# An exp split over two engines: VectorE's share as fp16 bits in six passes instead of seven, with an offset row in Q and K, and a new instruction order

## The chip, the cores and the metric

One core of one Trainium2 chip. The metric is the device time of one execution in microseconds, the median of several. Engines: PE is TensorE, DVE is VectorE, ACT is ScalarE.

## The reference

Two independent halves on inputs of 2048 x 640, joined at the end. Half A is a 2-D FFT filter, done in the kernel as chains of matmuls. Half B is attention with 32 heads of width 20:

```python
qkv = (x @ wqkv).reshape(B, S, 3, H, Dh)...          # H = 32, Dh = 20, S = 2048
scores = einsum("bhqd,bhkd->bhqk", q, k) * Dh ** -0.5
p = softmax(scores, axis=-1)
o = einsum("bhqk,bhkd->bhqd", p, v)
return o.transpose(...).reshape(B, S, D) @ wo
```

The exps of the softmax are the bulk: 32 x 2048 x 2048 of them, 2048 tiles of 128 keys by 512 queries.

## The kernel before

A scheduler in the program places every instruction of every engine in a fixed order, from estimated durations; the chip then runs each engine's queue in that order, with semaphores between them. PE makes scores of two or three tiles at a time into PSUM ("qk"), ACT takes their exp in one instruction into one of four SBUF buffers (PT), PE multiplies them with V ("PV") into one PSUM bank that belongs to the unit (four heads by 512 queries); at a unit's end DVE copies the bank out, and only then may the next unit's PV start. The exp on ACT, with scale and bias as immediates (the bias is the default 0):

```python
self.P.add("act", lambda e: e.activation(pt, in_, AF.Exp, scale=SCALE),
           r=[("ps", h + k) for k in range(n)], w=[("PT", i % 4)], name="exp")
```

DVE does some of the exps itself, two tiles at a time ("a pair"). It writes 1024*log2(e)*score as a uint16, corrects the fraction bits by a polynomial, and turns the sum into bits of a 16-bit float:

```python
# x_v: from PSUM, twice per pair
tensor_scalar(v, ps, 1024 * SCALE * LOG2E, 32 * 1024 + 512, mult, add)
# then on 128x1024 in SBUF, 16 bits:
x_s: sh = v << 6
x_t: t = sh * a + b                 # tensor_scalar
x_q: h = t * t                      # tensor_tensor
x_l: t = t * c + d                  # tensor_scalar
x_h: h = h * t                      # tensor_tensor
x_w: v = v + h                      # tensor_tensor
x_p: v = v * 0.125 + X_BIAS         # tensor_scalar: to bits of bf16
```

Evictions of Q and K from PSUM are plain casts (`copy_on`). All DVE jobs of half A (among them the complex multiply of stage FS2) are placed between these passes.

## Time and profile before

| | before |
|---|---|
| time, median | 916.43 us (915.7 to 918.68) |
| ACT busy | 839.7 us, of it exps 828.8 us (724 instructions) |
| DVE busy | 815.7 us |
| ACT idle ahead of exps | 53.4 us |
| granted PE clock, mean | 0.963 |

How to read it: in a group line, the first number after the bar is the union of the busy time, the second the mean duration of one instruction in ns, the third the idle time of its engine just before it and what ended most of it. Where records of one engine overlap, the union is less than count times duration. A hole is a stretch in which ACT waits. One piece of the trace belongs here: the 9.33 us hole, in time order (start, length, engine, line, operation).

```profile
564.09 0.61 PE L1265 MATMUL ps<-arena 128*128 128x512 bf16 x2 [2.58 <-DVE arena L227]
...
564.88 1.41 DVE L1253 TENSOR_TENSOR arena<-ps,arena 128x512 f32<-128x512 f32 x2
...
565.17 0.62 PE L1879 MATMUL ps<-arena 128*21 128x512 bf16 x4
566.21 0.68 DVE L1903 COPY arena<-ps 128x512 f32<-128x512 f32 x1
...
567.32 1.04 PE L1879 MATMUL ps<-arena 128*32 128x512 bf16 x8
...
567.99 1.45 ACT L1714 ACTIVATE arena<-ps 128x1536 bf16<-128x1536 f32 x1 [9.33 <-PE ps L1879]
```

Read it upwards. The exp waits for a PT buffer, which eight PVs of the new unit free (L1879). They wait for the copy of the old unit's bank (L1903). The copy comes after the old unit's last PVs (565.17) and, on DVE, after two multiplies of FS2 (L1253). Those PVs in turn stand on PE behind a matmul of half A (L1265), for which PE waited 2.58 us until DVE had done a cast (L227). So lateness on DVE, which is full of FS2 work, reaches ACT in steps, at a unit's end.

### The profile page before, as it was taken

To read this page: it belongs to the slowest core of one execution; us is meant where nothing else is said; L and a number is where in the kernel's file an instruction comes from. 1 tells how busy PE (TensorE), PEld (TensorE's weight loads), DVE (VectorE), ACT (ScalarE), POOL (GpSimd) and SP (SyncE) were. 2 spreads that over 40 slices of the span, in tenths; PEclk is the share of its full clock that TensorE was granted. 3 is DMA by queue.
4 is the path that set the end of the run, shared out by engine and by line. 5 is a ranking of instruction groups with operands and counts; after the bars stand their busy time and mean duration, and the time that the engine had idled before them with its cause. 6 is when DMAs were issued, how large, how long until landed. Compare 5 with 4: busy or idle time off the path is not lost.

```text
span 915.7 us, 16468 instructions
## 1 busy us (share of the span) xinstructions
PE 837.9 (92%) x6731; PEld 291.2 (32%) x6823; DVE 815.7 (89%) x1642; ACT 839.7 (92%) x744; POOL 2.9 (0%) x7
## 2 busy tenths in 40 slices
PE   8999999999899999999999997898899998989986
PEld 4433333333233333322233322223233332223222
DVE  5797799999799998999899999999999898678994
ACT  6898999998799999999999995999799999789993
POOL 1000000000000000000000000000000000000000
PEclk9999999999699999999999998999799999679999
DMA  7430000003200000011001000010010201011100
GB/s 228 87 82 14 2 14 13 14 14 93 73 28 27 13 14 13 14 48 36 13 20 35 13 13 1 13 59 14 1 59 20 78 13 42 1 41 43 42 13 32
DMA packets 31830, 31.85 MB, mean 35 GB/s; under 512 B 13444, under 2 KB 26500, under 8 KB 31492
## 3 DMA queue, kind: packets, MB, share of 16 engines
q1 hardware_dynamic: 31748, 30.73, 11.2%
q8 instruction: 55, 0.90, 0.4%
q14 instruction: 27, 0.22, 0.1%
HBM read 24.97 MB, written 5.50 MB: 33 GB/s over the span
## 4 chain that ended last, share of the span: by engine, by line
ACT 52%; PE 21%; DVE 20%; DMA 5%; issue 1%; SPq 0%; ACTq 0%; DVEq 0%
ACT arena L1714 51%; PE ps L1697 6%; DVE arena L227 4%; DMA arena<-rscr 4%; PE ps L1879 4%; DVE arena L1787 3%; DVE arena L1253 2%; PE ps L1331 2%; DVE arena L1828 1%; DVE arena L1835 1%; DVE arena L1832 1%; PE ps L1596 1%; DVE arena L1258 1%; PE ps L1533 1%; PE ps L1583 1%
## 5 line engine op out<-in xcount | busy, mean ns | idle before, releaser
L1714 ACT ACTIVATE arena<-ps 128x1536 bf16<-128x1536 f32 x724 | 828.8, 1276 | 53.4 <-PE ps L1697 28.2
L1697 PE MATMUL ps<-arena 32*128 32x512 bf16 x2048 | 309.3, 394 | 42.4 <-ACT arena L1714 22.5
L1879 PE MATMUL ps<-arena 128*32 128x512 bf16 (+1 forms) x2048 | 208.3, 401 | 5.0 <-DVE arena L1837 2.2
L1787 DVE TENSOR_SCALAR arena<-ps 128x512 uint16<-128x512 f32 x238 | 163.4, 687 | 30.6 <-PE ps L1697 28.4
L227 DVE CAST arena<-ps 128x512 bf16<-128x512 f32 (+4 forms) x248 | 143.7, 580 | 22.6 <-PE ps L1331 6.1
L1697 PEld LDWEIGHTS ps<-arena 32*128 32x128 bf16 x2048 | 74.3, 91 | 247.9 <-ACT arena L1714 180.7
L1879 PEld LDWEIGHTS ps<-arena 128*32 128x32 bf16 (+1 forms) x2048 | 51.3, 92 | 132.4 <-issue 107.6
L1583 PE MATMUL ps<-arena 128*128 128x512 bf16 x244 | 85.3, 397 | 3.5 <-issue 2.4
L1828 DVE TENSOR_TENSOR arena<-arena 128x1024 f16<-128x1024 f16 x119 | 81.8, 687 | 1.1
L1832 DVE TENSOR_TENSOR arena<-arena 128x1024 f16<-128x1024 f16 x119 | 81.9, 688 | 0.9
L1835 DVE TENSOR_TENSOR arena<-arena 128x1024 uint16<-128x1024 uint16 x119 | 81.5, 685 | 0.6
L1826 DVE TENSOR_SCALAR arena<-arena 128x1024 f16<-128x1024 int16 x119 | 50.4, 424 | 0.8
L1830 DVE TENSOR_SCALAR arena<-arena 128x1024 f16<-128x1024 f16 x119 | 50.1, 421 | 0.9
L1824 DVE TENSOR_SCALAR arena<-arena 128x1024 uint16<-128x1024 uint16 x119 | 50.1, 422 | 0.4
L1837 DVE TENSOR_SCALAR arena<-arena 128x1024 uint16<-128x1024 uint16 x119 | 50.1, 421 | 0.4
L1533 PE MATMUL ps<-arena 128*32 128x512 bf16 x640 | 47.8, 381 | 1.2 <-issue 0.5
L1596 PE MATMUL ps<-arena 128*128 128x512 bf16 x145 | 46.5, 396 | 1.5 <-issue 0.8
L1331 PE MATMUL ps<-arena 128*128 128x320 bf16 (+1 forms) x192 | 43.0, 330 | 4.3 <-DVE arena L1787 4.2
L227 DVE COPY arena<-ps 128x1024 bf16<-128x1024 bf16 (+2 forms) x55 | 40.2, 733 | 6.0 <-PE ps L540 4.6
L1583 PEld LDWEIGHTS ps<-arena 128*128 128x128 bf16 x317 | 26.7, 98 | 44.9 <-issue 39.3
L1964 PE MATMUL ps<-arena 128*128 128x320 bf16 x192 | 38.2, 303 | 0.1
L1942 DVE TENSOR_TENSOR arena<-arena 128x512 bf16<-128x512 f32 x31 | 21.4, 689 | 15.9 <-DMA arena<-rscr 15.4
(71 smaller groups left out, 464.3 us busy)
## 6 DMA issues: line engine op xcount, KB each, us to landing
arena<-rscr SPq DMA_DIRECT2D x31, 256.0 KB
arena<-in_B_x_dram SPq DMA_DIRECT2D x4, 640.0 KB, 6.4
arena<-in_A_x_dram SPq DMA_DIRECT2D x4, 640.0 KB, 6.2
out_dram<-arena SPq DMA_DIRECT2D x16, 160.0 KB, 1.8
out_dram<-arena SPq DMA_DIRECT2D x4, 640.0 KB, 3.4
arena<-f_ciCS SPq DMA_DIRECT2D x2, 1024.0 KB, 5.1
arena<-arena SPq DMA_DIRECT2D x124, 2.0 KB, 1.7
arena<-f_cslab SPq DMA_DIRECT2D x2, 768.0 KB, 4.4
```

The lines of the kernel that those rows point to most:

```text
L227: return eng.tensor_copy(out, in_)
L1331: return lambda e: e.matmul(o, l, r_, start=s_, stop=e_)
L1533: inst = e.matmul(ps[32 * j:32 * j + 32, bank, :], self.wqkv[:, cbv, c:c + 32], r_, start=st, stop=sp, tile_position=(0, 32 * j))
L1583: self.P.add("pe", lambda e: e.matmul(ps[:, 6, :], z, k[:, 0, 0:512], start=False, stop=False, skip_group_check=True), r=[("KT", 0, 0), (" ...
L1596: return lambda e: e.matmul(o, l, r_, start=st, stop=sp)
L1697: inst = e.matmul(ps[:, bank, :], kt_[32 * j:32 * j + 32, g, kt * 128:(kt + 1) * 128], q[32 * j:32 * j + 32, :], start=True, stop=True, ti ...
L1714: self.P.add("act", lambda e: e.activation(pt, in_, AF.Exp, scale=SCALE), r=[("ps", h + k) for k in range(n)], w=[("PT", i % 4)], name="exp")
L1787: self.P.add("dve", lambda e: e.tensor_scalar(v, in_, 1024.0 * SCALE * LOG2E, 32.0 * 1024 + 512, ALU.mult, ALU.add), r=[("ps", bank)], **( ...
L1828: t = self.x_op(n, two, lambda e: e.tensor_tensor(h16, t16, t16, ALU.mult), [ka], [kb], "x_q")
L1832: t = self.x_op(n, two, lambda e: e.tensor_tensor(h16, h16, t16, ALU.mult), [ka, kb], [kb], "x_h")
L1835: t = self.x_op(n, two, lambda e: e.tensor_tensor(v, v, h16, ALU.add), [kb, kv], [kv], "x_w")
L1879: inst = e.matmul(ps[32 * j:32 * j + m, 6, :], va[:, kt, 21 * h:21 * h + m], pt, start=st, stop=sp, tile_position=(0, 32 * j))
```

## The change

Its intent: take a pass off DVE, which is nearly full, by letting the scores carry an offset, so that x_v already gives the bits of fp16 (whose exponent bias is 15) and x_p falls away; and order the queues by measured durations. The offset is an added row, 1 in K and 46.5 in Q: 46.5 * SCALE is 15 in units of log2. ACT, which reads the same scores, takes it off again by its bias. The bias, and the scale and bias of the added row, come from columns of a small tile kq: one value for each of the 128 partitions, [128,1], in place of a constant in the instruction (an immediate).

```diff
+        kq[:, 0] = kq[:, 2] = 1.0
+        kq[20::32, 0:4] = (0.0, 1.0, 0.0, Y_ROW)     # scale, bias of K; scale, bias of Q
+        kq[:, 4] = -15.0 / LOG2E
...
+    def add_row(self, e, en, out, in_, c):           # replaces copy_on for Q and K
+        m, b = self.kq[:, c:c + 1], self.kq[:, c + 1:c + 2]
+        if en == "act":
+            return e.activation(out, in_, AF.Identity, bias=b, scale=m)
+        return e.tensor_scalar(out, in_, m, b, ALU.mult, ALU.add)
...
-        e.activation(pt, in_, AF.Exp, scale=SCALE)
+        e.activation(pt, in_, AF.Exp, scale=SCALE, bias=self.kq[:, 4:5])
...
-        x_v: ... 1024.0 * SCALE * LOG2E, 32.0 * 1024 + 512, ALU.mult, ALU.add
+        x_v: ... 1024.0 * SCALE * LOG2E, 31743.0, ALU.mult, ALU.min
...        (x_t, x_q, x_l, x_h: other coefficients; x_q is now uint16 * fp16)
-        elif step == 6: ... tensor_scalar(v, v, 0.125, X_BIAS, mult, add)    # x_p
...        (order)
-        FS2: 1.0417 * ne + 64               +  ... + 124 and + 144
-        UT evictions 0.52 ns an element     +  1.0417
-        job on DVE: sum + 40.0              +  sum + 3.0
+        a PV may start with fewer than four tiles when ACT would else be stuck
-        T_A=680000.0, WIN=1000.0, T_X=0.0, (wait for rb 3600.0)
+        T_A=760000.0, WIN=1400.0, T_X=40000.0, T_RB=9000.0
```

The names of the order part: FS2 and UT are stages of half A, "job on DVE" is what the scheduler adds to each DVE job; T_A paces half A, WIN is the stretch by which the scheduler decides on filler matmuls, T_X the earliest time of DVE's exps, T_RB the wait before a unit's normalization. The sums' certificate, a check of their range (max and min in two reduces, now one), changes too.

More of the change, by code (lines that the diff above doesn't have):

```diff
@@ L1122, in mkev @@
                         return lambda e, en: copy_on(e, en, o, in_)
-                    ev = [(mkev, 0.833 * n * 128 + 63, 0.52 * n * 128 + 64, [], [dst_key(c, b0 // 8)] + zwr, [])]
+                    ev = [(mkev, 0.833 * n * 128 + 63, (1.0417 if tag == "UT" else 0.52) * n * 128 + 64, [], [dst_key(c, b0 // 8)] + zwr, [])]
                     aft = after[c] if isinstance(after, dict) else after
@@ L1253, in mkev @@
                     return lambda e, en: e.tensor_tensor(t[k], ps[:, bank, 0:ne], w, ALU.mult)
-                return (mkev, 0.0, 1.0417 * ne + 64, kw, [("tmp", k)] + zw("K", 2), [])
+                return (mkev, 0.0, 1.0417 * ne + 124, kw, [("tmp", k)] + zw("K", 2), [])
             def comb(y, k0, k1, op, key, t=t):
@@ L1258, in mkev @@
                     return lambda e, en: e.tensor_tensor(y, t[k0], t[k1], op)
-                return (mkev, 0.0, 1.0417 * ne + 64, [("tmp", k0), ("tmp", k1), zr("K", 2)], [key] + zw("B", 3), [])
+                return (mkev, 0.0, 1.0417 * ne + 144, [("tmp", k0), ("tmp", k1), zr("K", 2)], [key] + zw("B", 3), [])
             for co in range(2):
@@ L1370 @@
 LOG2E = 1.4426950408889634
-X_K, X_BETA, X_GAMMA = 18.8641107, -0.0282624809, 0.224521806
-X_BIAS = 12084.9708
+Y_ROW = 46.5
+X_A, X_B = 0.30457565, 0.07826797
 MODE = 100.0
 SLACK = 200.0
+F16 = mybir.dt.float16
 DMA_NS = 2200.0
@@ L1415, in alloc @@
         self.outB = [a.bf(take(1280), 640) for _ in range(2)]
-        self.rin = a.f32(take(64), 16)
-        self.rc = a.f32(take(64), 16)
+        self.rr = a.f32(take(128), 32)
+        self.rin, self.rc = self.rr[:, 0:16], self.rr[:, 16:32]
+        self.kq = a.f32(take(32), 8)
         self.mm = a.f32(take(256), 64)
         self.cert = a.f32(take(32), 8)
-        self.flagt = a.f32(take(32), 8)
+        self.flagt = self.cert[:, 6:8]
         self.vmx = a.f32(take(64), 16)
@@ L1462, in setup_B @@
         self.dma(self.ident, cBd.ap(), w=[("ident",)], name="ld_ident")
+        kq = np.zeros((128, 8), np.float32)
+        kq[:, 0] = kq[:, 2] = 1.0
+        kq[20::32, 0:4] = (0.0, 1.0, 0.0, Y_ROW)
+        kq[:, 4] = -15.0 / LOG2E
+        kqd = self.nc.inline_tensor(kq, self.prefix + "kq")
+        self.dma(self.kq, kqd.ap(), w=[("kq",)], name="ld_kq")
         xB = self.B_x[0].rearrange("(t p) c -> p t c", p=128)
@@ L1539, in mk_jobs_B_static, with mkev @@
                 J.pe = pe
+                def mkev(bank, g=g, kc=kc):
+                    o = self.KT[:, g, kc * 512:(kc + 1) * 512]
+                    return lambda e, en: self.add_row(e, en, o, ps[:, bank, :], 0)
+                J.ev = [(mkev, 490.0, 600.0, [("kq",)], [("KT", g, kc)], [])]
                 J.mode = "c"
@@ L1600, in mkev @@
             o = self.QA[u % 2]
-            in_ = ps[:, bank, :]
-            return lambda e, en: copy_on(e, en, o, in_)
-        ev = [(mkev, 490.0, 598.0, [], [("QA", u % 2)], [])]
+            return lambda e, en: self.add_row(e, en, o, ps[:, bank, :], 2)
+        ev = [(mkev, 490.0, 600.0, [("kq",)], [("QA", u % 2)], [])]
         cond = lambda p: g in self.wq_done and (u < 2 or self.qk_left[u - 2] == 0)
@@ L1713, in try_exp @@
         in_ = self.ps[:, h:h + n, :].rearrange("p b n -> p (b n)")
-        self.P.add("act", lambda e: e.activation(pt, in_, AF.Exp, scale=SCALE),
-                   r=[("ps", h + k) for k in range(n)], w=[("PT", i % 4)], name="exp")
+        self.P.add("act", lambda e: e.activation(pt, in_, AF.Exp, scale=SCALE, bias=self.kq[:, 4:5]),
+                   r=[("ps", h + k) for k in range(n)] + [("kq",)], w=[("PT", i % 4)], name="exp")
         t = self.occupy("act", 512 * n * 0.8333 + 50.0, 0.0)
@@ L1786, in try_x_first @@
         key = ("xv", n % NXV)
-        self.P.add("dve", lambda e: e.tensor_scalar(v, in_, 1024.0 * SCALE * LOG2E, 32.0 * 1024 + 512, ALU.mult, ALU.add),
+        self.P.add("dve", lambda e: e.tensor_scalar(v, in_, 1024.0 * SCALE * LOG2E, 31743.0, ALU.mult, ALU.min),
                    r=[("ps", bank)], **({"w": [key]} if k == 0 else {"pw": [key]}), name="x_v")
@@ L1808, in try_x_step @@
             self.x_step(c)
-            if c[1] == 7:
+            if c[1] == 6:
                 self.x_run.remove(c)
@@ L1815, in x_step @@
         n, step, t, pair = c
-        I16, F16 = mybir.dt.int16, mybir.dt.float16
         kv, ka, kb = ("xv", n % NXV), ("xa", n % 2), ("xb", n % 2)
         xv, xa, xb = self.xv[n % NXV], self.xa[n % 2], self.xb[n % 2]
-        v, sh, g = xv.bitcast(U16), xa.bitcast(U16), xa.bitcast(I16)
-        t16, h16 = xa.bitcast(F16), xb.bitcast(F16)
+        v, sh = xv.bitcast(U16), xa.bitcast(U16)
+        a16, b16 = xa.bitcast(F16), xb.bitcast(F16)
         one, two = 336.0, 603.0
@@ L1825, in x_step @@
         elif step == 1:
-            t = self.x_op(n, one, lambda e: e.tensor_scalar(t16, g, X_K / 65536.0, X_K * X_BETA, ALU.mult, ALU.add), [ka], [ka], "x_t")
+            t = self.x_op(n, one, lambda e: e.tensor_scalar(b16, sh, -2.0 ** -24, 2.0 ** -8, ALU.mult, ALU.add), [ka], [kb], "x_l")
         elif step == 2:
-            t = self.x_op(n, two, lambda e: e.tensor_tensor(h16, t16, t16, ALU.mult), [ka], [kb], "x_q")
+            t = self.x_op(n, two, lambda e: e.tensor_tensor(b16, sh, b16, ALU.mult), [ka, kb], [kb], "x_q")
         elif step == 3:
-            t = self.x_op(n, one, lambda e: e.tensor_scalar(t16, t16, X_GAMMA / X_K, 1.0 - X_GAMMA * X_BETA, ALU.mult, ALU.add), [ka], [ka], "x_l")
+            t = self.x_op(n, one, lambda e: e.tensor_scalar(a16, sh, -4.0 * X_B / 65536.0, -4.0 * X_A, ALU.mult, ALU.add), [ka], [ka], "x_l")
         elif step == 4:
-            t = self.x_op(n, two, lambda e: e.tensor_tensor(h16, h16, t16, ALU.mult), [ka, kb], [kb], "x_h")
+            t = self.x_op(n, two, lambda e: e.tensor_tensor(b16, b16, a16, ALU.mult), [ka, kb], [kb], "x_h")
             self.xa_free[n % 2] = t
         elif step == 5:
-            t = self.x_op(n, two, lambda e: e.tensor_tensor(v, v, h16, ALU.add), [kb, kv], [kv], "x_w")
-        elif step == 6:
-            t = self.x_op(n, one, lambda e: e.tensor_scalar(v, v, 0.125, X_BIAS, ALU.mult, ALU.add), [kv], [kv], "x_p")
+            t = self.x_op(n, two, lambda e: e.tensor_tensor(v, v, b16, ALU.add), [kb, kv], [kv], "x_w")
             for k, (u, kt, j) in enumerate(pair):
-                self.pv_ready[u].append((t + SLACK, kt, j, xv[:, 512 * k:512 * k + 512], kv))
+                self.pv_ready[u].append((t + SLACK, kt, j, xv.bitcast(F16)[:, 512 * k:512 * k + 512], kv))
             self.at(t + SLACK)
@@ L1860, in try_pv @@
                 break
-        if len(pick) < min(least, self.pv_left[u]):
+        heads = sum(self.pv_cnt.get((u, j), 0) < 16 for j in range(4))
+        i = self.nexp
+        stuck = i < self.nqk and self.qk_t[i] <= self.now and self.pt_free[i % 4] > self.now + 1e9 and self.tf["act"] <= self.now
+        if len(pick) < (1 if stuck else min(least, heads)):
             return False
@@ L1921, in unit_recip @@
         P.add("dve", lambda e: e.reciprocal(rc, rin), r=[("rin",)], w=[("rc",)], name="recip")
-        m0, m1 = self.mm[:, 2 * u:2 * u + 1], self.mm[:, 2 * u + 1:2 * u + 2]
-        P.add("dve", lambda e: e.tensor_reduce(m0, rin, AX.X, ALU.max), r=[("rin",)], pw=[("mm",)], name="smax")
-        P.add("dve", lambda e: e.tensor_reduce(m1, rin, AX.X, ALU.min), r=[("rin",)], pw=[("mm",)], name="smin")
-        t = self.occupy("dve", 400.0)
+        m, both = self.mm[:, 2 * u:2 * u + 2], self.rr.rearrange("p (c e) -> p c e", c=2)
+        P.add("dve", lambda e: e.tensor_reduce(m, both, AX.X, ALU.max), r=[("rin",), ("rc",)], pw=[("mm",)], name="sums")
+        t = self.occupy("dve", 270.0)
         rs = self.rscr[u]
@@ L1934, in d2 @@
             self.dma(rb, src, r=[("rs", u)], w=[("rb",)], stream="rb", name="rb")
-            self.dve_urgent.append((self.now + 3600.0, lambda: self.unit_norm(u), lambda: self.op_left[:u // NG].count(0) == u // NG))
-            self.at(self.now + 3600.0)
+            self.dve_urgent.append((self.now + self.cfg["T_RB"], lambda: self.unit_norm(u), lambda: self.op_left[:u // NG].count(0) == u // NG))
+            self.at(self.now + self.cfg["T_RB"])
         self.at(t, d1)
@@ L2031, in tail_norm @@
         if qb == 3:
-            m0, m1, ball = self.mm[:, 62:63], self.mm[:, 63:64], self.ps[:, 5, :]
-            self.P.add("dve", lambda e: e.tensor_reduce(m0, ball, AX.X, ALU.max), r=[("ps", 5)], pw=[("mm",)], name="smax")
-            self.P.add("dve", lambda e: e.tensor_reduce(m1, ball, AX.X, ALU.min), r=[("ps", 5)], pw=[("mm",)], name="smin")
+            m0, m1, ball, inv = self.mm[:, 62:63], self.mm[:, 63:64], self.ps[:, 5, :], self.rb
+            self.P.add("dve", lambda e: e.tensor_reduce(m0, ball, AX.X, ALU.max), r=[("ps", 5)], pw=[("mm",)], name="sums")
+            self.P.add("dve", lambda e: e.tensor_reduce(m1, inv, AX.X, ALU.max), r=[("rb",)], pw=[("mm",)], name="sums")
     def tail_act(self):
@@ L2141, in try_bg_ev @@
                            r=[("ps", J.bank)] + list(rk), w=wk, pw=pk, name=J.name + ".ev")
-            t = self.occupy(en, sum(x[1 if en == "act" else 2] for x in J.ev) + 40.0)
+            t = self.occupy(en, sum(x[1 if en == "act" else 2] for x in J.ev) + (40.0 if en == "act" else 3.0))
             J.done_p = t
@@ L2305, in emit_flag @@
         ps = self.ps
-        LO, HI = 2.0 ** -8, 2.0 ** 31
-        P.add("dve", lambda e: e.tensor_reduce(c[:, 0:1], mm, AX.X, ALU.max), r=[("mm",)], w=[("c", 0)], name="cmax")
-        P.add("dve", lambda e: e.tensor_reduce(c[:, 1:2], mm, AX.X, ALU.min), r=[("mm",)], w=[("c", 1)], name="cmin")
+        both = mm.rearrange("p (u c) -> p c u", c=2)
+        P.add("dve", lambda e: e.tensor_reduce(c[:, 0:2], both, AX.X, ALU.max), r=[("mm",)], w=[("c", 0)], name="csum")
         P.add("dve", lambda e: e.tensor_reduce(c[:, 2:3], self.vmx, AX.X, ALU.max), r=[("vmx",)], w=[("c", 2)], name="cv")
-        P.add("dve", lambda e: e.tensor_single_scalar(c[:, 3:4], c[:, 0:1], HI, ALU.is_gt), r=[("c", 0)], w=[("c", 3)], name="f0")
-        P.add("dve", lambda e: e.tensor_single_scalar(c[:, 4:5], c[:, 1:2], LO, ALU.is_lt), r=[("c", 1)], w=[("c", 4)], name="f1")
-        P.add("dve", lambda e: e.tensor_single_scalar(c[:, 5:6], c[:, 2:3], 2.0 ** 60, ALU.is_gt), r=[("c", 2)], w=[("c", 5)], name="f2")
+        P.add("dve", lambda e: e.tensor_single_scalar(c[:, 3:4], c[:, 0:1], 65000.0, ALU.is_le), r=[("c", 0)], w=[("c", 3)], name="f0")
+        P.add("dve", lambda e: e.tensor_single_scalar(c[:, 4:5], c[:, 1:2], 2.0 ** -6, ALU.is_le), r=[("c", 0)], w=[("c", 4)], name="f1")
+        P.add("dve", lambda e: e.tensor_single_scalar(c[:, 5:6], c[:, 2:3], 2.0 ** 60, ALU.is_le), r=[("c", 2)], w=[("c", 5)], name="f2")
         o1 = self.ones1
@@ L2315, in emit_flag @@
               r=[("c", 3), ("c", 4), ("c", 5), ("ones1",)], w=[("ps", 7)], name="fsum")
-        P.add("dve", lambda e: e.tensor_reduce(fl[0:1, 1:2], ps[0:1, 7, 0:3], AX.X, ALU.max), r=[("ps", 7)], w=[("fl", 1)], name="fmax")
+        P.add("dve", lambda e: e.tensor_reduce(fl[0:1, 1:2], ps[0:1, 7, 0:3], AX.X, ALU.min), r=[("ps", 7), ("c", 5)], w=[("fl", 1)], name="fmin")
         fi = fl.bitcast(mybir.dt.int32)[0:1, 0:1]
-        self.flag_task = P.add("dve", lambda e: e.tensor_single_scalar(fi, fl[0:1, 1:2], 0.0, ALU.is_gt), r=[("fl", 1)], w=[("fl", 0)], name="flag")
+        self.flag_task = P.add("dve", lambda e: e.tensor_single_scalar(fi, fl[0:1, 1:2], 127.5, ALU.is_lt), r=[("fl", 1)], w=[("fl", 0)], name="flag")
         self.flag = fi
@@ L2341, in bass_concat_heads__spectral_gfnet__softmax_full_mha__prompt_kernel @@
     arena = Arena(nc, 212832 - 64)
-    fast = FK(nc, arena, *args, cfg=dict(LEAD=20, T_A=680000.0, WARM_SHARE=0.45, RUN=2, PVQ=8, WIN=1000.0, T_X=0.0, AHEAD=45e3))
+    fast = FK(nc, arena, *args, cfg=dict(LEAD=20, T_A=760000.0, WARM_SHARE=0.45, RUN=2, PVQ=8, WIN=1400.0, T_X=40000.0, AHEAD=45e3, T_RB=9000.0))
     fast.build()
```

## The prediction

> **What bounds the kernel now.** I read the page first (engine totals, slices, chain), then the waits, then ACT's order in time and a table by stretch of 40 us. The page:
>
> ```profile
> span 915.7 us, 16468 instructions
> PE 837.9 (92%) x6731; PEld 291.2 (32%) x6823; DVE 815.7 (89%) x1642; ACT 839.7 (92%) x744; POOL 2.9 (0%) x7
> ...
> ACT  6898999998799999999999995999799999789993
> ...
> PEclk9999999999699999999999998999799999679999
> ...
> ACT 52%; PE 21%; DVE 20%; DMA 5%; issue 1%; SPq 0%; ACTq 0%; DVEq 0%
> ...
> L1714 ACT ACTIVATE arena<-ps 128x1536 bf16<-128x1536 f32 x724 | 828.8, 1276 | 53.4 <-PE ps L1697 28.2
> ...
> L1787 DVE TENSOR_SCALAR arena<-ps 128x512 uint16<-128x512 f32 x238 | 163.4, 687 | 30.6 <-PE ps L1697 28.4
> L1828 DVE TENSOR_TENSOR arena<-arena 128x1024 f16<-128x1024 f16 x119 | 81.8, 687 | 1.1
> ...
> L1835 DVE TENSOR_TENSOR arena<-arena 128x1024 uint16<-128x1024 uint16 x119 | 81.5, 685 | 0.6
> ...
> L1837 DVE TENSOR_SCALAR arena<-arena 128x1024 uint16<-128x1024 uint16 x119 | 50.1, 421 | 0.4
> ```
>
> There are 2048 score tiles (32 heads x 16 x 4). ACT takes 1810 of them in 724 exps (362 of three tiles, 362 of two), VectorE 238 in 119 pairs. The ACT row is at 9 in most slices, and half of the chain is the exps: **ACT is the bound**, and DVE and PE share the chain only where ACT starves. In time order, ACT's first exp starts at 14.27 us and its last ends at 898.69; the tail after that is 17.0 us. Between the two lie 828.8 us of exps, 2.4 us of four copies, and some 53 us of idle. So 916 = 14.3 + 829 + 2.4 + 53 + 17. The 53 us are all that a better order or a lighter DVE can win, unless exps change hands or length.
>
> Where the 53 us lie, from the waits, ACT's order in time and the stretches:
>
> ```profile
> ACT arena L1714 <- PE ps L1697: 28.2, 37, 2.0
> ...
> ACT arena L1714 <- PE ps L1879: 23.4, 16, 9.3
> ```
>
> ```profile
> 444.15 114.51 ACT L1714 ACTIVATE arena<-ps 128x1536 bf16<-128x1536 f32 x100 [0.16 <-PE ps L1697]
> 567.99 2.36 ACT L1714 ACTIVATE arena<-ps 128x1536 bf16<-128x1536 f32 x2 [9.33 <-PE ps L1879]
> ```
>
> ```profile
> 400.00:440.00 40.00, 37.50 (x264) 11.28 (x268) 37.53 (x83) 40.00 (x37) 0.00 (x0) 1.00 0.11 34
> ...
> 560.00:600.00 40.00, 33.34 (x204) 9.30 (x208) 36.77 (x63) 30.18 (x27) 0.00 (x0) 0.91 0.03 8
> ...
> 760.00:800.00 40.00, 36.51 (x227) 11.19 (x231) 29.43 (x65) 31.89 (x28) 0.00 (x0) 0.79 0.08 25
> ```
>
> In the last view the columns are the busy time of PE, weight loads, DVE, ACT, GpSimd, then the granted clock. Two kinds of hole are seen. **DVE holes**: 100 exps run without a gap, then 9.33 us are lost. Just before that hole, PE stands for 2.58 us at a matmul of the other branch, waiting for DVE, which is in the FS2 stage (L1253, L1258); PE runs its queue in order, so scores queued behind it come late. **Clock holes**: at 237-254, 568-575, 646-656, 780-796 and 814-824 us the granted clock is 0.5, and ACT has holes in the same places (about 27 us of the 53); in 760-800 DVE isn't even full.
>
> **What the Trainium skill says.** (1) "VectorE: DVE Perf Modes", the perf-mode tier table: 16-bit tensor_scalar in SBUF runs at 4x, tensor_tensor at 2x. The trace agrees: L1837 and L1835, both 1024 elements, take 421 and 685 ns, and (685-421) ns is close to the 267 ns between 1024/2 and 1024/4 cycles at its 0.96 GHz. (2) "TensorE: Matmul & The Clock Gate", Part 1: TensorE's clock halves after an idle window and comes back after a busy one. The trace agrees: five windows at 0.5 besides the end, of 3.4 us and multiples. (3) "ScalarE: Activation LUTs", What ACT_TABLE_LOAD costs: an ACTIVATE with immediate scale and bias takes 186 ns plus 0.833 ns an element, and each [128,1] pointer operand adds about 93 ns. The trace has only the immediate form: 1487 ns at 1536 and 1066 ns at 1024 elements are 0.82 ns an element plus about 210. Nothing here shows the pointer form.
>
> **The change, part by part.**
>
> *VectorE's exp.* The program's order has the same 119 pairs as before. Each pair loses L1837, 421 ns: 119 x 421 = 50.1 us of records. Consecutive DVE records overlap by some 0.09 us (a 421 ns record is followed after 0.33), so 119 x 0.33 = 39 us of DVE time. The other six passes keep their shape and 16-bit types. The one that multiplies a uint16 by an fp16 could have fallen to a slower mode; but L1835 already adds a uint16 and an fp16 tensor at 685 ns, so I expect 687 ns again. The new first pass is still one tensor_scalar from PSUM (multiply and min for multiply and add): 687 ns.
>
> *Row of Q and K.* 64 evictions of 128x512 become scale-and-bias with per-partition operands, 62 on DVE at about 687 ns, as the plain casts. DVE takes four more of them than before, 4 x 0.61 = 2.4 us, and ACT four fewer, which takes 2.4 us off ACT early on. One small load more at the start, before a 4.8 us wait that is there anyway: nothing.
>
> *Sums and certificate.* Two tensor_reduces (114 and 155 ns) become one of some 160: 31 x 0.1 = 3 us of DVE. In the tail, one reduce fewer of the flag: 0.1 us.
>
> DVE then has some 39 + 3 - 2 = 40 us less to do, and ACT exactly as many exps as before: 362 + 362. So 40 us on DVE are worth only what they close of ACT's holes.
>
> *Order.* I counted DVE's instructions, in the order in which the program was recorded, between every 36 exps, priced by start-to-start times of the trace (0.33, 0.60 and 0.61 us for the passes, 0.65 for L1253, 1.1 for the transposing copies). 36 exps take 36 x 1.145 = 41.2 us. Before, five stretches ask DVE for more: 43.0 at the start, 46.6 (exps 144-180), 49.9, 44.4 and 45.2 (exps 432-540, the FS2 stage), altogether 23 us over. After, four do: 42.9, 43.2, 43.8, 42.4, altogether 7.5 us over, and the first stretches ask 26 and 30 because VectorE's exps start only at 40 us. So the DVE holes (about 20 us with their small followers) should fall by two thirds. The longer wait before the normalization (9.0 for 3.6 us) takes away DVE's own 15.4 us of waiting for the broadcast (L1942), which is no hole of ACT by itself.
>
> *Clock.* The fillers fall from 341 to 290 while the window that decides on them grows from 1.0 to 1.4 us. Fewer stalls of PE make fewer dips, fewer fillers make more; I let them fall from 27 to about 18 us of holes.
>
> Sum without a change of the exp's own length: 14 + 829 + 0 + (7 DVE + 18 clock + 7 small) + 17 = 893 us; with luck either way 880 to 905.
>
> *The bias of the exp.* Every exp now reads its bias, -10.4, from a [128,1] column instead of an immediate 0. This is the one cost that falls on the bound. If the 93 ns of the skill fall between exps, they are 724 x 93 = 67 us; if part is hidden, as 1487 + 1066 - 2 x 1145 = 263 ns of each pair of records are hidden now (131 each), then less.
>
> **The rivals.** A: the pointer's read is hidden behind the exp before it; then about 893. For it: back-to-back exps already overlap by 131 ns, more than the 93; and the change speaks of an order recalibrated by the trace, and left the order's cost of an exp alone, which 8% longer exps would hardly have allowed. B: it is exposed, 60 to 93 ns each: 43 to 67 us on ACT, of which slacker DVE and PE give back some holes (32 down to 22): 925 to 950. For B: the skill's wording, and that each exp now pays a fixed 78 ns beyond its 1280 x 0.833, so the overlap looks like the tail of the writes, not a prefetch of reads. C: DVE's relief is real, but new dips of the clock take it back: 905 to 915; for it speaks that half of the holes come with the clock, and that 51 fillers go.
>
> **How the range follows.** A and C together I give 0.62, centred at 893 with 9 us to either side, B 0.38, centred at 938. Under 898.1 (faster by 2%) lie three quarters of the first: 0.48. Between 898.1 and 934.8: the rest of it and two fifths of B, 0.29. Above: 0.23. The time I name, 895, leans to the first; the range, 881 to 943, takes in most of B.
>
> **What would show it.** The exp group: 1487 and 1066 ns against 1580 and 1160, and above all a run of 100 exps without a hole: 114.5 us under A, 121 to 124 under B. DVE's busy time should fall to about 765 us, all six passes at 421 to 424 or 685 to 690 ns. The hole of 9.33 us should be gone or under 4 us; ACT's idle ahead of exps should be 25 to 40 us. The dips to 0.5 should be at most five. Wrong would make it: a mixed multiply at over 1 us (+60 us on DVE, which then bounds); the certificate failing, which adds the whole slow program, over 1000 us; or holes staying at 50 us though DVE is lighter.

## More of the kernel before

Three executions fell in a slower state: one of a_imm_p7, named there, and two of the kernel before that ran beside it. Ratios leave them out.

## The result, and the profile after

The changed kernel takes 930.63 us (930.22 to 932.75), beside 917.55 us of the kernel before in the same rounds: ratio 1.0147, 95% interval 1.0117 to 1.0176. A ratio is the mean time of one kernel's fast runs over that of the other's of the same rounds, so not quite the ratio of the medians quoted. **Slower by 1.5%**, a small loss but clear of the scatter, though DVE does less and ACT starves less.

The same lines as in the prediction, of the profile after: totals, slices, chain, groups.

```profile
span 929.1 us, 16296 instructions
PE 832.4 (90%) x6772; PEld 285.6 (31%) x6772; DVE 798.6 (86%) x1495; ACT 894.7 (96%) x740; POOL 2.9 (0%) x7
...
ACT  6999999999998999999999999999999999999994
...
PEclk9999999999999999999999999999999999999999
...
ACT 91%; PE 7%; DMA 1%; issue 0%; SPq 0%; DVE 0%; ACTq 0%
...
L1734 ACT ACTIVATE arena<-ps,arena 128x1536 bf16<-128x1536 f32 x724 | 885.4, 1397 | 13.1 <-PE ps L1717 6.6
...
L1808 DVE TENSOR_SCALAR arena<-ps 128x512 uint16<-128x512 f32 x238 | 163.6, 688 | 43.5 <-PE ps L1717 40.9
...
L1848 DVE TENSOR_TENSOR arena<-arena 128x1024 f16<-128x1024 uint16 x119 | 81.4, 686 | 1.3
...
L1508 DVE TENSOR_SCALAR arena<-ps,arena 128x512 bf16<-128x512 f32 x62 | 50.0, 807 | 18.4 <-PE ps L1549 11.4
```

The ACT row is at 9 from end to end, the granted clock dips to 0.5 only once ahead of the tail (3.4 us, before six times), idle ahead of exps fell from 53.4 to 13.1 us, and the chain is ACT for 91% instead of 52%. What was hoped for of the holes happened. But the same 724 exps are busy for 885.4 instead of 828.8 us, and their input list has got a second name ("arena"): the bias column. By form, and in a stretch without a hole (ACT's order in time):

```profile
L1734 ACT ACTIVATE arena<-ps,arena 128x1536 bf16<-128x1536 f32 x362 | 582.4, 1609 | 9.0 <-PE ps L1717 5.6 <-PE ps L1900 3.0
L1734 ACT ACTIVATE arena<-ps,arena 128x1024 bf16<-128x1024 f32 x362 | 429.2, 1186 | 4.2 <-PE ps L1900 2.9 <-PE ps L1717 1.0
```

```profile
302.80 205.33 ACT L1734 ACTIVATE arena<-ps,arena 128x1536 bf16<-128x1536 f32 x168 [3.25 <-PE ps L1717]
```

205.33 / 168 is 1.222 us an exp, against 1.145 before (114.51 / 100). The span follows: exps busy 56.6 us longer, idle between first and last exp 40.3 us less, four copies (2.4 us) moved to DVE, the first exp 0.3 us later, the tail 0.5 us shorter: 56.6 - 40.3 - 2.4 + 0.3 - 0.5 = 13.7, measured 929.1 - 915.7 = 13.4 us.

### The profile page after: what moved, and what is told of

The parts are those of the page before. It is cut to its first block, busy times and chain, and to the rows that moved or that the text cites. A ratio compares the mean times of both kernels' runs of the same rounds, so it can differ in the third digit from the quotient of the medians.

```text
span 929.1 us, 16296 instructions
## 1 busy us (share of the span) xinstructions
PE 832.4 (90%) x6772; PEld 285.6 (31%) x6772; DVE 798.6 (86%) x1495; ACT 894.7 (96%) x740; POOL 2.9 (0%) x7
## 4 chain that ended last, share of the span: by engine, by line
ACT 91%; PE 7%; DMA 1%; issue 0%; SPq 0%; DVE 0%; ACTq 0%
ACT arena L1734 91%; PE ps L1717 2%; PE ps L1900 1%; PE ps L2011 1%; DMA arena<-in_B_x_dram 1%; PE ps L1549 1%; PE ps L1577 1%; PE ps L1617 0%; PE ps L1984 0%; PE ps L1604 0%; SPq L362 0%; PE ps L2012 0%; ACT arena L2062 0%; PE ps L1230 0%; PE ps L2024 0%
## 5 line engine op out<-in xcount | busy, mean ns | idle before, releaser
L1734 ACT ACTIVATE arena<-ps,arena 128x1536 bf16<-128x1536 f32 x724 | 885.4, 1397 | 13.1 <-PE ps L1717 6.6
L1900 PE MATMUL ps<-arena 128*32 128x512 bf16 (+3 forms) x2048 | 202.7, 389 | 2.2 <-ACT arena L1734 1.2
L1808 DVE TENSOR_SCALAR arena<-ps 128x512 uint16<-128x512 f32 x238 | 163.6, 688 | 43.5 <-PE ps L1717 40.9
L227 DVE CAST arena<-ps 128x320 bf16<-128x320 f32 (+4 forms) x190 | 104.1, 548 | 25.6 <-PE ps L1577 10.9
L1848 DVE TENSOR_TENSOR arena<-arena 128x1024 f16<-128x1024 uint16 x119 | 81.4, 686 | 1.3
L1852 DVE TENSOR_TENSOR arena<-arena 128x1024 f16<-128x1024 f16 x119 | 81.5, 685 | 1.2
L1508 DVE TENSOR_SCALAR arena<-ps,arena 128x512 bf16<-128x512 f32 x62 | 50.0, 807 | 18.4 <-PE ps L1549 11.4
L1850 DVE TENSOR_SCALAR arena<-arena 128x1024 f16<-128x1024 uint16 x119 | 50.1, 422 | 1.1
L1846 DVE TENSOR_SCALAR arena<-arena 128x1024 f16<-128x1024 uint16 x119 | 49.9, 421 | 1.1
L1844 DVE TENSOR_SCALAR arena<-arena 128x1024 uint16<-128x1024 uint16 x119 | 50.0, 422 | 0.6
L227 DVE COPY arena<-ps 128x1024 bf16<-128x1024 bf16 (+2 forms) x55 | 40.2, 734 | 11.4 <-PE ps L540 6.9
L1577 PE MATMUL ps<-arena 128*128 128x80 bf16 (+1 forms) x320 | 33.2, 236 | 0.1
L1253 DVE TENSOR_TENSOR arena<-ps,arena 128x512 f32<-128x512 f32 (+1 forms) x44 | 28.8, 653 | 4.6 <-PE ps L1265 3.6
```

The source lines that it names most:

```text
L227: return eng.tensor_copy(out, in_)
L1508: return e.tensor_scalar(out, in_, m, b, ALU.mult, ALU.add)
L1808: self.P.add("dve", lambda e: e.tensor_scalar(v, in_, 1024.0 * SCALE * LOG2E, 31743.0, ALU.mult, ALU.min), r=[("ps", bank)], **({"w": [key ...
L1848: t = self.x_op(n, two, lambda e: e.tensor_tensor(b16, sh, b16, ALU.mult), [ka, kb], [kb], "x_q")
L1850: t = self.x_op(n, one, lambda e: e.tensor_scalar(a16, sh, -4.0 * X_B / 65536.0, -4.0 * X_A, ALU.mult, ALU.add), [ka], [ka], "x_l")
L1852: t = self.x_op(n, two, lambda e: e.tensor_tensor(b16, b16, a16, ALU.mult), [ka, kb], [kb], "x_h")
```

## The experiments

**Theory:** the [128,1] column given as the exp's bias costs some 80 ns on every exp, on the engine that bounds the kernel; without it the change is a gain. **Rivals:** the exps are longer because of their new neighbours (order, DVE passes) or because of the bias's value; or the change isn't a gain even without the column.

| run | edit | time, us | ratio to before (95%) | exps, idle ahead of them |
|---|---|---|---|---|
| before | | 917.55 | 1 | 724, 53.4 us |
| after | | 930.63 | 1.0147 (1.0117 to 1.0176) | 724, 13.1 us |
| a_imm | after, bias as immediate | 877.0 | 0.9563 (0.9537 to 0.9589) | 724, 17.9 us |
| b_ptr | before, bias as column | 964.02 | 1.0503 (1.0468 to 1.0539) | 724, 40.6 us |
| a_ptr2 | after, scale as column too | 1001.47 | 1.0927 (1.0891 to 1.0964) | 724, 11.8 us |
| a_scale | after, scale as column, bias immediate | 930.52 | 1.0161 (1.0110 to 1.0212) | 724, 12.5 us |
| b_order | before, new order | 895.3 | 0.9760 (0.9729 to 0.9792) | 731, 34.4 us |
| a_imm_old | a_imm, old order | 903.62 | 0.9867 (0.9808 to 0.9926) | 721, 40.9 us |
| a_imm_p7 | a_imm, a seventh pass again | 920.74 | 1.0038 (0.9972 to 1.0105) | 724, 52.2 us |
| v_cal | a_imm, order recalibrated further | 893.71 | 0.9762 (0.9709 to 0.9815) | 719, 41.0 us |
| v_tx15 | a_imm, DVE's exps from 15 us | 889.34 | 0.9709 (0.9659 to 0.9760) | 720, 32.9 us |
| a_imm_q1 | a_imm, one column in Q's evictions | 875.99 | 0.9558 (0.9522 to 0.9594) | 724, 17.3 us |

All experiments gave correct results. The median of before, rerun beside each set, lay between 916.0 and 918.5 us. In a_imm, b_ptr, a_ptr2, a_scale, a_imm_p7 and a_imm_q1 the order of the instructions is exactly that of the kernel they come from (a_imm_p7 with its added pass); the sequences of DVE and ACT in the traces agree.

### a_imm: one operand

```diff
-            e.activation(pt, in_, AF.Exp, scale=SCALE, bias=self.kq[:, 4:5])
+            e.activation(pt, in_, AF.Exp, scale=SCALE, bias=-15.0 / LOG2E)
```

(With the operand, the wait for its load goes too; that is one wait at the start.)

> The changed kernel with one operand changed: the exp's bias is an immediate of the same value (-10.397) in place of the [128,1] column; the order of all instructions and the results stay the same. Theory (the column costs about 77 ns on every exp, 56 us in all): exp records fall back to 1487 and 1066 ns, a run without holes to 1.145 us an exp, time 875 to 890 us. Rival (the exps are longer because of what DVE and PE do beside them now, or because of the value of the bias): records stay at 1609 and 1186 ns, time 925 to 932 us.

877.0 us (875.66 to 877.48): 4.4% faster than before, and 5.8% under the changed kernel by the medians. The records are back at their old length, and the chain is 54% ACT, 29% DVE:

```profile
L1734 ACT ACTIVATE arena<-ps 128x1536 bf16<-128x1536 f32 x362 | 538.5, 1488 | 13.2 <-PE ps L1717 7.7 <-PE ps L1900 3.9
L1734 ACT ACTIVATE arena<-ps 128x1024 bf16<-128x1024 f32 x362 | 386.0, 1066 | 4.8 <-PE ps L1900 3.5 <-PE ps L1717 1.2
```

```profile
684.24 84.04 ACT L1734 ACTIVATE arena<-ps 128x1536 bf16<-128x1536 f32 x74 [0.83 <-PE ps L1900]
```

84.04 / 74 is 1.136 us an exp. Same value of the bias, same neighbours, same order: it is the column. This one operand turns a gain of 4.4% into a loss of 1.5%.

### b_ptr: the column alone, in the kernel before

```diff
+        P.add("pool", lambda e: e.memset(zb[:, 6:7], 0.0), w=[("zb",)], ...)
-            e.activation(pt, in_, AF.Exp, scale=SCALE)
+            e.activation(pt, in_, AF.Exp, scale=SCALE, bias=self.cert[:, 6:7])
```

> The kernel before with one operand changed: the exp's bias 0 comes from a [128,1] column of zeros in place of an immediate; order and results stay the same. Theory (the column's read is exposed): a hole-free run at 1.222 us an exp instead of 1.145, +56 us on ACT, of which slacker DVE gives back 20 to 40 us of the holes: 930 to 955 us. Rival (the pointer is not the cause): 914 to 920 us and records of 1487 and 1066 ns.

964.02 us, longer than the 930 to 955 expected. The bias is 0 here and the order is the old one, and still the exps are busy for 887.3 us, 58.5 us more than before (81 ns each): neither the value of the bias nor the new neighbours are needed. The group here, and two exps that follow each other right after a wait, in the kernel before and here (0.19 us more for the two):

```profile
L1716 ACT ACTIVATE arena<-ps,arena 128x1536 bf16<-128x1536 f32 x724 | 887.3, 1400 | 40.6 <-PE ps L1881 20.3
```

```profile
652.10 2.36 ACT L1714 ACTIVATE arena<-ps 128x1536 bf16<-128x1536 f32 x2 [1.21 <-PE ps L1697]
```

```profile
679.33 2.55 ACT L1716 ACTIVATE arena<-ps,arena 128x1536 bf16<-128x1536 f32 x2 [1.02 <-PE ps L1699]
```

The slower ACT closed only 12.8 us of the holes, not 20 to 40. With the column, the new order and six passes only 13.1 us are left (the changed kernel); with the column, the old order and seven passes it is 40.6 us. This run leaves open which of the two, order or passes, closed them; b_order and a_imm_old below take them apart.

### a_ptr2 and a_scale: is it each column, or the bias?

```diff
 a_ptr2:   AF.Exp, scale=self.kq[:, 5:6], bias=self.kq[:, 4:5]
 a_scale:  AF.Exp, scale=self.kq[:, 5:6], bias=-15.0 / LOG2E
```

> The changed kernel with the exp's scale from a [128,1] column too: two pointer operands in each exp, same order and results. Theory (each column is read by itself ahead of the stream): another 60 to 95 ns an exp, 724 times: 972 to 1000 us. Rival (one access fetches all columns, or the second hides behind the first): 928 to 936 us.

> The changed kernel with the exp's scale from a [128,1] column and its bias as an immediate: one column again, but the other operand; same order and results. If any one column costs the same, a hole-free run takes 1.218 to 1.225 us an exp and the time is 927 to 934 us, as with the bias column. If the second column measured before (another 90 ns) was dearer because it was the scale, 1.23 to 1.24 us and 938 to 945 us.

The second column adds about as much again: 1001.47 us, just over the 972 to 1000 expected (six executions from 995.08 to 1008.1 us, the four longer ones at a lower clock, 0.968 to 0.983 against 0.991 and 0.994). And one column costs the same whether it is the scale or the bias (930.52 against 930.63 us, records 1609 and 1186 ns in both). The exps of a_ptr2 by form:

```profile
L1735 ACT ACTIVATE arena<-ps,arena 128x1536 bf16<-128x1536 f32 x362 | 623.1, 1721 | 8.0 <-PE ps L1718 5.7 <-PE ps L1901 2.0
L1735 ACT ACTIVATE arena<-ps,arena 128x1024 bf16<-128x1024 f32 x362 | 469.6, 1297 | 3.9 <-PE ps L1901 2.8 <-PE ps L1718 1.0
```

Busy time of the 724 exps is 825.7, 885.4 and 950.6 us with no, one and two columns: 82 ns for the first and 90 ns for the second. These means also hold exps that start somewhat late without a gap that the views would show as idle. The start times in the traces show the cost without them. After an exp of three tiles the next one starts, in the median, 1331 ns later in a_imm, 1424 in the changed kernel and 1515 in a_ptr2; after one of two tiles it is 904, 997 and 1089 ns. So each column costs 91 to 93 ns between exps that follow each other, the first nearly the same as the second, and the same at 1024 and at 1536 elements: a fixed cost per instruction. The shortest records grow by no more (two tiles: 1017, 1106 and 1194 ns), so nothing of it hides behind the exp before. What the starts lie further apart than these medians, gaps and small delays together, adds up to 34 us in a_imm, 22 us in the changed kernel and 20 us in a_ptr2: with slower exps ACT loses less elsewhere. So the first column costs 723 x 93 ns = 67 us less some 12 us, that is 55 us, which is the difference of the spans (929.1 - 873.8).

### b_order and a_imm_old: order and arithmetic apart

b_order is the kernel before with only the "order" part of the diff; a_imm_old is a_imm with that part undone.

```diff
 b_order (on before), the other way round in a_imm_old (on a_imm):
- FS2 + 64, UT 0.52, job on DVE + 40.0, PV only with four tiles
- T_A=680000.0, WIN=1000.0, T_X=0.0, wait for rb 3600.0
+ FS2 + 124 and + 144, UT 1.0417, job on DVE + 3.0, PV with fewer when ACT would be stuck
+ T_A=760000.0, WIN=1400.0, T_X=40000.0, T_RB=9000.0
```

> The kernel before with its own arithmetic (seven passes on the pair, no row, immediate bias) but the new order: the recalibrated costs, the new settings and the new rule for PV. The scheduler gives it 731 exps and 111 pairs (before 724 and 119). If the holes of ACT were an error of the order alone, idle ahead of the exps falls from 53 to 25 us or less and the time to 890 to 900 us; if they needed the pass less on DVE, idle stays over 40 us and the time at 910 to 925 us.

> The change's arithmetic (six passes, the row of Q and K) with an immediate bias, but the order and settings of the kernel before; the scheduler gives it 721 exps and 123 pairs. If the new order is what closed ACT's holes (with the old arithmetic it brought 918 to 895), idle ahead of the exps stays at 35 us or more, the clock dips return, and the time is 890 to 905 us. If the pass less on DVE closes them by itself, idle is 15 to 25 us and the time 870 to 882 us.

With immediates throughout, the four corners are (median, us):

| | old order | new order |
|---|---|---|
| seven passes, no row | 917.6 | 895.3 |
| six passes, row | 903.6 | 877.0 |

The order is worth 22 to 27 us, the arithmetic 14 to 18 us, and they nearly add (the scheduler hands out 719 to 731 exps as it sees fit, so a corner holds a few us of that too). Against both expectations in detail: idle of b_order is 34.4 us (expected 25 or less, or over 40), with one dip of the clock of 20.5 us left; a_imm_old kept 40.9 us of holes and landed at the upper end of its first range. The dips of the clock ahead of the tail: the profiled run of before has six, that of the changed kernel one of 3.4 us, a_imm none, a_imm_old three, b_order one, and b_ptr, in the old order with ACT as slow as in the changed kernel, six. They don't follow the order alone: a_imm_p7 (next section), in a_imm's order with one pass more, has four. In the 3.4 us ahead of each of the six in before, PE stood for 1.0 to 2.6 us. That fits a clock that halves where PE stands, and then lengthens the holes, but the 3.4 us from 438.9 us, in which PE stood for 1.6 us, brought no dip, and no run changed the clock alone.

### a_imm_p7: what the removed pass is worth by itself

```diff
+            self.P.add("dve", lambda e: e.tensor_single_scalar(f, f, 1.0, ALU.mult), r=[kv], w=[kv], name="x_p")
```

> The changed kernel with an immediate bias and, on each pair, a seventh pass again (multiply by 1.0, 1024 elements of fp16 in place): the same order, the same results, 119 more DVE instructions of 421 ns. It prices the removed pass alone, 39 us of DVE time. If DVE's slack absorbs it, the time stays within 4 us of the run with the immediate bias (877 us). If DVE is close to the bound in the middle of the kernel, holes come back in the FS2 stage and between exps 100 and 180: 885 to 905 us.

920.74 us (median of four, one of them at 936.49 and not counted in the ratio), longer than the 885 to 905 of its second case: 44 us more than a_imm, a little over the whole 119 x 0.33 = 39 us of DVE time. Its chain:

```profile
DVE 71%; ACT 14%; PE 12%; issue 2%; ACTq 0%; DVEq 0%
```

In a_imm, then, DVE is no longer slack: put the pass back without a new order, and DVE sets the end. (The order was made for six passes, so this overstates what the pass is worth when the scheduler may react: then pass and row together were 18 us, table above.)

### v_cal, v_tx15, a_imm_q1: tries for a better version

```diff
 v_cal:    exp 512 * n * 0.8333 + 50.0  ->  + 78.0 ;  evictions with columns on DVE 600.0 -> 730.0
 v_tx15:   T_X=40000.0 -> T_X=15000.0
 a_imm_q1: Q's eviction: tensor_scalar(out, in_, m, b, mult, add) -> tensor_single_scalar(out, in_, b, add)
```

> A try for a better version: immediate bias, and the order calculated with what the traces show (78 ns instead of 50 for the fixed part of an exp, 730 ns instead of 600 for an eviction with two column operands on DVE). The scheduler gives 719 exps and 126 pairs. ACT has 5 exps less (6 us) and the idle of 18 us may fall a little: 866 to 875 us. Rival: the extra 7 pairs (28 us of DVE) make holes of their own: 877 to 885 us.

> A try for a better version: immediate bias, VectorE's exps from 15 us on instead of 40. The scheduler gives 720 exps and 124 pairs: 4 exps less are 4.6 us. Theory: DVE has idle time at the start (its busy tenths there are 3 4 8 7), so 870 to 875 us. Rival: early pairs delay the evictions that the first scores need, and ACT starves at the start: 877 to 890 us.

> A try for a better version, and a measure of a column on VectorE: immediate bias in the exp, and the 32 evictions of Q only add their column (the rows that get the offset hold zeros before it, so no scale is needed), one column in place of two; the 32 evictions of K keep two. Same order and results. If DVE pays for each column, as ACT does, those of Q fall from 806 to about 745 ns and DVE has 2 us less: 874 to 877 us, hardly to be told from 877. If it pays once for both, they stay at 806 ns.

Both new orders lost 12 to 17 us, though they give ACT 4 or 5 exps less: a miss, v_cal beyond its rival's range too, v_tx15 within it (877 to 890), though the largest part of its loss is not at the start. In v_cal most of it is two holes, in the FS2 stage and after it:

```profile
531.11 3.28 ACT L1734 ACTIVATE arena<-ps 128x1024 bf16<-128x1024 f32 x3 [14.39 <-PE ps L1900]
593.58 16.92 ACT L1734 ACTIVATE arena<-ps 128x1024 bf16<-128x1024 f32 x15 [9.08 <-PE ps L1900]
```

At the first, the trace shows the picture of the hole in before: the unit's last PVs, the copy of its bank at 529.34 us, eight PVs of the next unit, the exp. v_tx15 has one such hole of 9.23 us. In each of these holes, as in that of before, PE stood at the matmul L1265 for a cast on DVE (L227): 2.58 us in before, 2.55 and 2.81 in v_cal, 1.99 in v_tx15. I did not find out which setting keeps the hole away. Nor was v_cal a test of truer durations: its 78 ns come from hole-free runs, which hold small delays. Exps that follow each other start, in the median, 1331 and 904 ns apart, 50 ns more than 0.833 ns an element, which is the scheduler's old figure and close to the some 51 ns of engine time per ScalarE instruction on PSUM that the Trainium skill states ("Perfetto Trace Analysis", Optimizing Scalar/DVE Operations).

a_imm_q1 is as fast as a_imm within the scatter (875.99 us). DVE pays for each column: the evictions of Q (L1509) fell from 805 to 744 ns, those of K (L1512) stayed at 805.

```profile
L1512 DVE TENSOR_SCALAR arena<-ps,arena 128x512 bf16<-128x512 f32 x31 | 24.9, 805 | 9.6 <-PE ps L1553 9.6
...
L1509 DVE TENSOR_SCALAR arena<-ps,arena 128x512 bf16<-128x512 f32 x31 | 23.1, 744 | 4.5 <-PE ps L1621 4.3
```

## Why the prediction was wrong

- **The bound and the sum of the kernel before** (14.3 + 829 + 2.4 + 53 + 17): right, and the same sum explains the result.
- **DVE's passes:** right. L1837 is gone, the mixed multiply takes 686 ns, the first pass 688 ns, and there are still 724 exps and 119 pairs.
- **Evictions with the row:** wrong by a size. "At about 687 ns, as the plain casts" measured 807 ns: two columns cost DVE 120 ns, 62 times, 7 us. DVE's busy time of 798.6 us instead of 765 holds these 7 us; the rest is overlap lost, since records that no longer follow back to back count in full: the records overlap by 81 us in all, before by 108 (with ACT faster, in a_imm, the same instructions are busy for 785.5 us). The 765 also took off the removed records whole, 50 us, where the prediction itself had counted 39.
- **Order and holes:** right in direction, too careful in size. With the bias out of the way the holes were 17.9 us, not 32: no dip of the clock was left in a_imm, where 18 us of holes had been allowed for them. So the change without the column makes 877, not 893 us. Rival C, that fewer fillers bring the dips back, fell. In the readings, before had six dips, not "five" (one of 3.4 us at 735.6 us was overlooked), and the times given for them are 3 us late (233.8 to 250.9, not "237-254"). Ahead of them PE stood for 1.0 to 2.6 us of 3.4 us, so the "idle window" that it cites is not seen whole in this trace, and the trace decides. And in the 9.33 us hole ACT waited for PVs that free its buffer (L1879), not for scores.
- **The bias of the exp:** the step that failed. The prediction saw the operand, and gave the right size for rival B: "60 to 93 ns each", 121 to 124 us for 100 exps (measured 122.2), 925 to 950 us (measured 930.6). But it gave B 0.38 and put 895 as the time, on rival A: that the pointer's read is hidden behind the exp before it. That is the step, and the runs showed the opposite: between exps that follow each other the column costs 93 ns (1331 to 1424, 904 to 997), all of the 93 ns cited, with nothing hidden; 12 of these 67 us came back in fewer gaps and delays. The two grounds for A did not hold. That records "already overlap by 131 ns, more than the 93" says nothing about which part of the next instruction lies in the overlap. And that the order "left the order's cost of an exp alone" was a guess about how the settings came to be, not a reading of the profile: its 50 ns are right for the immediate form between exps that follow each other, and about 143 would have been right for the column. (The prediction's "fixed 78 ns", a ground for B, holds small delays.)
- **What was luck:** the range of 881 to 943 holds the result because it was drawn around both rivals. And B's centre, 938, came near only because two errors partly cancel: A's 893 was 16 us too high for the kernel without the column (877), and B's cost less the holes given back, 45 us, was 9 too low (54).
- **Slips in the sums**, without effect on the outcome: 14 + 829 + 32 + 17 is 892, not 893; three quarters of 0.62 are 0.465, not 0.48; and 1487 and 1066 ns at 0.82 ns an element leave about 224 ns, not 210.
- So the main term, 56 to 60 us of busy time, was in the text and was weighed too low. A cost on every instruction of the bound engine deserves more weight than a hope that it hides.

What stays open: where in the instruction the column is read (only that its time is exposed is shown); which setting makes or avoids the large holes of the FS2 stage; and what the dips of the clock are worth by themselves.

## What to carry to other kernels

Look at the operand list of each instruction on the engine that bounds the kernel: a per-partition column where an immediate would do was 54 us here by the medians, more than the pass and the new row's arithmetic saved (14 to 18 us). When a change that takes work off one engine brings nothing, see whether it put a small fixed cost on the other. And test such a cost by swapping only the operand, with order and values the same.

## What the Trainium skill lacked or had wrong

- "ScalarE: Activation LUTs", What ACT_TABLE_LOAD costs: it gives about 93 ns for each [128,1] operand and about 93 ns of overlap of back-to-back ACTIVATEs, and doesn't say whether the one hides in the other. Here, reading PSUM and writing SBUF, it doesn't: starts of exps that follow each other lie 93 ns further apart with one column and 91 to 92 more with the second. The records grow by more in the mean (121 and 112 ns), the busy time by less (82 and 90 ns an exp).
- "VectorE: DVE Perf Modes", Scalar operands: it describes [P, 1] operands without a price. From PSUM, 128x512: 685 ns with two immediates (L1808 in a_imm), 744 ns with one column, 805 ns with two, so about 60 ns each.
